# wo's last slice on 16 partitions by two loads, in a decode step of grouped-query attention with an MLP

## The chip, the cores and the metric

The kernel runs on one core of one Trainium2 chip. The metric is the device time of one execution in microseconds (us). Engines are named as the profile names them: PE (TensorE) with its weight loads PEld, DVE (VectorE), ACT (ScalarE), POOL (GpSimd) and SP, which here only issues transfers; 16 DMA engines move the data.

## The reference

One token x (512 values) goes through a layer norm, then through two branches whose results are added to x. All is float32.

```
xn = layernorm(x)
A:  q = xn @ wq                      # 32 heads of 128, wq 512 x 4096
    scores = q . k_cache * 128**-0.5  # 8 key heads, 65536 keys of 128 each; 4 query heads share one
    o = softmax(scores) @ v_cache
    a = concat(o) @ wo               # wo 4096 x 512
B:  b = relu(xn @ w1) @ w2           # w1 512 x 1792, w2 1792 x 512
out = x + a + b
```

k_cache and v_cache are 256 MiB each; wq and wo are 8 MiB each, w1 and w2 3.5 MiB each. All of it is read once.

## The kernel before

The arrays are laid out so that every transfer has long rows. SP issues all large loads, in this order: wq into the buffer `vs` in two loads, the first 8 MiB of k into the buffer `ks`; then in turn 8 MiB of v into `vs` and 8 MiB of k into `ks`, 32 of each (8 heads, four steps a head). A load waits until its buffer is free again: `k_free` is given by DVE when it has read the last score tile (L373), `v_free` by DVE when PE's sums of a step are complete (L396). While one buffer is computed on, the other is being filled.

When the last k buffer is free, w1 and w2 go into `ks`, still ahead of the last step's sums. When the last v buffer is free, wo goes into `vs`. wo is laid out with partition p = 16h + i (head group h, i from 0 to 15), and on each partition lie 32 slices of 512 values: slice j = 4r + g holds wo's row for head 4h + g and position 8i + r. `load_slices` cuts the 32 slices into loads of 16, 8, 4, 2, 1 and 1 (`WO`).

The end of the kernel is written out in order, with a semaphore for each engine (`Flow.op` waits for the marks that it is given, then issues). PE computes the MLP's hidden layer (L441), merges the heads (L451 to L464) and gathers w2 into acc_z (14 gathers). The attention output is spread by a matmul with `octet` (L483), masked and summed to `sw` (L485, L492): column j of `sw` holds, for each partition, the value that multiplies slice j. A *gather* (L503) is one matmul of a weight column with a row of 512; its result, one row, goes to one of four partitions of acc_z (0, 32, 64, 96, in turn), so that four gathers lie on four parts of the array.

acc_z's four rows must at the end become one, and the 512 results must go to four rows of 128 in acc_y, from which one transpose on DVE (L546) makes the layout of the output. Slices 0 to 27 (`DIRECT` is 28) are gathered in acc_z. Then DVE copies acc_z to `rows` (L534, called the fold's copy below). Slices 28 to 31 go straight into acc_y, four matmuls of 128 columns for each (L538). The fold's four matmuls with ones (L523) stand in PE's order behind slice 29, so that the copy runs beside the direct slices 28 and 29. After slice 31 the transpose and the output transfer follow.

On PE each of these matmuls shows as two instructions and two weight loads in the profile, so x8 in a row is four gathers, or one direct slice.

The functions that the change touches follow, with the line numbers of the profile.

Of the kernel before, what the change touches and what calls it, by code (L numbers as in the profile page):

```python
# [15 lines left out]
P = 128  # L16
D = 512
HQ, HKV, DH = 32, 8, 128
SK = 65536
DFF = 1792  # L20
G = HQ // HKV
CT = 4
# [12 lines left out]
R = HKV  # L35
SLICES = R * G
WQ = [4, 28]
WO = [16, 8, 4, 2, 1, 1]
DIRECT = 28
EPS = 1e-5  # L40

# [27 lines left out]
def attention_and_mlp_kernel(  # L69
# [30 lines left out]
    te, ve, se, ge, sy = nc.tensor, nc.vector, nc.scalar, nc.gpsimd, nc.sync  # L100

    def place(name, *shape, rows=P):
        return nc.alloc_sbuf_tensor(name, [rows, *shape], F32).ap()
# [9 lines left out]
    x4, yt = place("x4", P), place("yt", 32, 4)  # L113
    sw = place("sw", SLICES)
    mine = place("mine", HKV)
    octet = place("octet", P)
    eighth = place("eighth", R)

# [20 lines left out]
    rows = place("rows", 512)  # L139
# [10 lines left out]
    PE, DV, AC, GP = (Flow(nc, e, n) for e, n in ((te, "pe"), (ve, "dve"), (se, "act"), (ge, "pool")))  # L150

    def load(engine, name, dst, src, n=16):
        sem = nc.alloc_semaphore(name)
        engine.dma_start(dst, src).then_inc(sem, n)  # L154
        return sem, n


    def load_slices(name, src, counts):
        marks = []
        for n in counts:  # L160
            cut = slice(len(marks) * D, (len(marks) + n) * D)
            marks += [load(sy, f"{name}{len(marks)}", vs[:, cut], src[:, cut])] * n
        return marks
# [7 lines left out]
    tc.compile()  # L171


    make_identity_marks = []

    def memset(flow, ap, value):
        return flow.op(lambda e: e.memset(ap, value))

# [4 lines left out]
    for t in (acc_o, acc_z, pm):  # L183
# [9 lines left out]
        g0,  # L193
    )
    made = GP.mark
    x4_in = None
    se.wait_ge(*x4_free)
    x4_in = load(se, "x4_in", x4[0:P:32, :], x.rearrange("(c n) -> c n", c=CT))
# [43 lines left out]
            octet[:, : P // R].unsqueeze(1).to_broadcast([P, HKV - 1, P // R]),  # L242
        ),
        DV.mark,
    )
    DV.op(
        lambda e: e.tensor_mul(
# [4 lines left out]
    pz = pb[:, 1, :]  # L252
# [23 lines left out]
    for i in range(SLICES):  # L276
# [4 lines left out]
                start=(i < CT), stop=(i >= SLICES - CT),  # L281
# [34 lines left out]
    t1, t2 = ks[:, : A * DFF], ks[:, A * DFF : A * DFF + FB * D]  # L316
    w1_in = load(sy, "w1_in", t1, w1.rearrange("p a f -> p (a f)"))
    w2_in = load(sy, "w2_in", t2, w2.rearrange("p j n -> p (j n)"))
    sy.wait_ge(v_free, 1)
    wo_in = load_slices("wo", wo.rearrange("h (i r) g f -> (h i) (r g f)", r=R), WO)  # L320

# [14 lines left out]
    with nc.Fori(0, STEPS, engines=[ENG.PE]):  # L336
        te.wait_ge(k_in, 16).then_inc(k_in, -16)
        te.wait_ge(q_in, 1).then_inc(q_in, -1)  # L338
        for s in range(NT):
            tile_of = (pa, pb)[s // 2 % 2][:, s % 2, :]  # L340
            for c in range(CT):
                at = (s * CT + c) * TW
                i = te.matmul(tile_of[32 * c : 32 * c + 32, :], qcur, ks[:, at : at + TW], start=True, stop=True)  # L343
# [13 lines left out]
        for i in range(n):  # L357
# [5 lines left out]
                start=(i < CT), stop=(i >= n - CT),  # L363
# [4 lines left out]
    with nc.Fori(0, HKV, engines=[ENG.DVE], hint_back_edge=True, head_slot={ENG.DVE: 110}):  # L368
        for n in range(NP):
            for s in range(0, NT, 2):  # L370
                if s == NT - 2:

                    ve.wait_ge(s_tiles, NT // 2).then_inc(k_free, 1)  # L373
                i = ve.transpose(  # L374
                    tr[:, s * SUB : (s + 2) * SUB, :].rearrange("p b i -> p (b i)"),
                    (pa, pb)[s // 2 % 2].rearrange("p i k -> p (i k)"),
                )._wait_ge(s_tiles, s // 2 + 1)
# [5 lines left out]
            i = ve.reduce_max(top, tr[:, :, :G].rearrange("p b g -> p g b"), axis=AX.X)  # L383
            if n:
                ve.drain()
                i = ve.tensor_max(m, m, mc)  # L386
# [29 lines left out]
    with nc.Fori(0, HKV, engines=[ENG.Activation]):  # L416
        for n in range(NP):
            se.wait_ge(s_bias, 1).then_inc(s_bias, -1)  # L418
            for g in range(G):
                i = se.activation(  # L420
                    wt[:, :, g], tr[:, :, g], AF.Exp, bias=bias[:, n, g : g + 1],
                    scale=scale, accum_out=part[:, n, g : g + 1],
                )
# [13 lines left out]
    for a in range(A):  # L437
        for c in range(CT):
# [4 lines left out]
                    start=(a == 0), stop=(a == A - 1),  # L443
# [18 lines left out]
    for j in range(2):  # L462
# [28 lines left out]
    sw_in = DV.op(  # L491
        lambda e: e.reduce_sum(  # L492
            sw.rearrange("p (r g) -> p r g", r=R), spread.rearrange("p r h g -> p r g h"), axis=AX.X
        ),
        DV.mark,
    )

    begun = set()

    def gather(c, lhsT, row, marks, last=False):  # L500

        PE.op(
            lambda e: e.matmul(acc_z[32 * c : 32 * c + 1, :], lhsT, row, start=c not in begun, stop=last),  # L503
            *marks,
        )
        begun.add(c)
# [7 lines left out]
        )  # L514
    for j in range(FB):
        gather(j % CT, hT[:, j : j + 1], t2[:, j * D : (j + 1) * D], [hT_in, w2_in])

    for j in range(SLICES):
        if j == SLICES - 2:

            for c in range(CT):
                PE.op(
                    lambda e: e.matmul(  # L523
                        acc_y[32 * c : 32 * c + 1, :P], ones[:, 0:1], rows[:, c * P : (c + 1) * P],
                        start=False, stop=False,
                    ),
                    folded,
                )
        row = vs[:, j * D : (j + 1) * D]
        lhsT = sw[:, j : j + 1]  # L530
        if j < DIRECT:
            gather(j % CT, lhsT, row, [sw_in, wo_in[j]], last=(j >= DIRECT - CT))
            if j == DIRECT - 1:
                folded = DV.op(lambda e: e.tensor_copy(rows, acc_z), PE.mark)  # L534
        else:
            for c in range(CT):
                PE.op(
                    lambda e: e.matmul(  # L538
                        acc_y[32 * c : 32 * c + 1, :P], lhsT, row[:, c * P : (c + 1) * P],
                        start=False, stop=(j == SLICES - 1),  # L540
                    ),
                    sw_in, wo_in[j],
                )
# [40 lines left out]
```

## Time and profile before

| | us |
|---|---|
| median of 3 runs | 1303.35 (1303.03 to 1304.14) |
| the profiled execution | 1303.55 |
| its span, first to last instruction | 1302.2 |
| PE busy in it | 660.5 (51%) |
| DVE busy in it | 268.3 (21%) |
| ACT busy in it | 76.0 (6%) |
| bytes read from HBM in it | 560.99 MB, 431 GB/s over the span |

The mean granted clock of PE in this execution was 0.726 of full speed. In the rows below, times count from the first instruction of the span. A row of the timeline gives start, duration, engine, line, operation, output and inputs, shapes, the number of instructions merged in it, and in brackets the idle time of the engine before it with what ended it. A row of windows gives a stretch, its length, PE's busy time, PE's granted clock, the busy share of the 16 DMA engines and the GB/s that they moved. A row of a DMA queue gives its packets, its MB and the share of the 16 engines' time in that stretch.

### The profile page before, as it was taken

What the parts mean: (1) busy time and instruction counts of PE and PEld (TensorE: products, weight loads), DVE (VectorE), ACT (ScalarE), POOL (GpSimd) and SP (SyncE); (2) the same over time, 40 slices, a digit from 0 to 9 for tenths busy, and PEclk for the clock granted to TensorE, in tenths of its full rate; (3) what the DMA queues carried; (4) which work ended last, traced back from release to release, by engine and by line L of the source; (5) the groups of instructions that cost most, each with busy time, mean ns of one, the idle gap of its engine ahead of it and who ended that gap; (6) DMA issues with size and microseconds to landing.
All of it is one profiled execution on the core that took longest, in us unless ns stands there. A gap on an engine that the chain in (4) does not pass through costs nothing. (4 is left out here: it accounts for less than half of the span.)

```text
span 1302.2 us, 10668 instructions
## 1 busy us (share of the span) xinstructions
PE 660.5 (51%) x4512; PEld 184.9 (14%) x4512; DVE 268.3 (21%) x398; ACT 76.0 (6%) x292; POOL 4.1 (0%) x22
## 2 busy tenths in 40 slices
PE   3355455445445445546545535645544644544557
PEld 1111111111111111111111111111111111111111
DVE  2221122221122222012222112222112222201222
ACT  0000000000000000000000000000000000000000
POOL 0000000000000000000000000000000000000000
PEclk9677777687677677677667667677767767666768
DMA  9999999999999999999999999999999999999998
GB/s 417 421 443 425 445 425 439 431 425 445 423 447 421 449 419 445 425 445 425 433 437 425 445 421 449 421 447 421 445 425 439 431 431 439 423 447 421 449 416 360
DMA packets 10956, 561.06 MB, mean 431 GB/s; under 512 B 1476, under 2 KB 1480, under 8 KB 1864
## 3 DMA queue, kind: packets, MB, share of 16 engines
q1 hardware_dynamic: 10800, 561.00, 99.6%
q8 instruction: 3, 0.05, 0.0%
q10 hardware_dynamic: 152, 0.00, 0.0%
q14 instruction: 1, 0.01, 0.0%
HBM read 560.99 MB, written 0.00 MB: 431 GB/s over the span
## 5 line engine op out<-in xcount | busy, mean ns | idle before, releaser
L359 PE MATMUL acc_o<-vs,wt 128*16 128x512 f32 x2048 | 293.8, 738 | 178.9 <-PEq L355 178.9
L343 PE MATMUL pa<-ks,qcur 128*32 128x512 f32 x1024 | 175.7, 819 | 324.9 <-PEq L338 324.9
L374 DVE STREAM_TRANSPOSE tr<-pa 128x1024 f32<-128x1024 f32 x64 | 80.0, 1250 | 413.1 <-PE pa L343 413.1
L343 PE MATMUL pb<-ks,qcur 128*32 128x512 f32 x1024 | 139.6, 664 | 0.0
L420 ACT ACTIVATE wt<-tr,bias 128x128 f32<-128x128 f32 x128 | 64.3, 511 | 1083.7 <-ACTq L418 1083.7
L359 PEld LDWEIGHTS acc_o<-vs,wt 128*16 128x16 f32 x2048 | 69.0, 113 | 377.0 <-issue 377.0
L343 PEld LDWEIGHTS pa<-ks,qcur 128*32 128x32 f32 x1024 | 38.8, 134 | 432.7 <-issue 424.4
L400 DVE SCALAR_TENSOR_TENSOR acc<-acc,alpha,acc_o 128x512 f32<-128x512 f32 x24 | 17.9, 748 | 352.7 <-PE acc_o L359 352.7
L374 DVE STREAM_TRANSPOSE tr<-pb 128x1024 f32<-128x1024 f32 x64 | 80.0, 1250 | 49.6 <-PE pb L343 49.6
L343 PEld LDWEIGHTS pb<-ks,qcur 128*32 128x32 f32 x1024 | 41.6, 131 | 107.0 <-issue 87.9
L348 PE MATMUL pm<-ident,m 128*4 128x128 f32 x32 | 10.4, 324 | 87.7 <-DVE m L386 67.2
L398 DVE COPY acc<-acc_o 128x512 f32<-128x512 f32 x8 | 5.5, 691 | 119.3 <-PE acc_o L359 119.3
L349 PE MATMUL pm<-dg,ones 4*128 4x4 f32 x64 | 15.8, 316 | 21.3 <-DVE dg L390 21.3
L383 DVE TENSOR_REDUCE mc<-tr 128x4 f32<-128x512 f32 x24 | 24.1, 1006 | 1.8
L420 ACT ACTIVATION_READ_ACCUMULATOR wt<-tr,bias 128x1 f32 x128 | 23.9, 187 | 0.0
L348 PEld LDWEIGHTS pm<-ident,m 128*4 128x4 f32 x32 | 2.6, 81 | 116.7 <-DVE m L386 89.0
L349 PEld LDWEIGHTS pm<-dg,ones 4*128 4x128 f32 x64 | 13.0, 253 | 29.1 <-DVE dg L390 29.1
L350 PE MATMUL pm<-dg,rowg 4*128 4x1 f32 x64 | 15.1, 302 | 0.0
L279 PE MATMUL pa<-vs,tr 128*8 128x512 f32 x64 | 10.4, 809 | 8.6 <-DMA vs<-wq 7.3
L350 PEld LDWEIGHTS pm<-dg,rowg 4*128 4x128 f32 x64 | 13.9, 266 | 0.0
L388 DVE TENSOR_REDUCE mg<-pm 4x1 f32<-4x128 f32 x32 | 8.9, 279 | 13.3 <-PE pm L348 13.3
L391 DVE COPY bias<-pm 128x5 f32<-128x5 f32 x32 | 5.2, 163 | 29.5 <-PE pm L350 29.5
(98 smaller groups left out, 99.2 us busy)
## 6 DMA issues: line engine op xcount, KB each, us to landing
vs<-wq SPq DMA_DIRECT2D x1, 7168.0 KB, 21.2
ks<-w SPq DMA_DIRECT2D x2, 3584.0 KB, 21.8
vs<-wo SPq DMA_DIRECT2D x1, 4096.0 KB, 17.9
vs<-wo SPq DMA_DIRECT2D x1, 2048.0 KB, 22.4
vs<-wq SPq DMA_DIRECT2D x1, 1024.0 KB, 4.7
vs<-wo SPq DMA_DIRECT2D x1, 1024.0 KB, 24.4
ks<-k SPq DMA_DIRECT2D x32, 29.0
vs<-v SPq DMA_DIRECT2D x32, 28.9
```

Of the source, the lines that this page charges most:

```text
L279: lambda e: e.matmul(pr[32 * c : 32 * c + HKV, :], xs[:, i, :], vs[:, i * 512 : (i + 1) * 512], start=(i < CT), stop=(i >= SLICES - CT),),
L343: i = te.matmul(tile_of[32 * c : 32 * c + 32, :], qcur, ks[:, at : at + TW], start=True, stop=True)
L348: te.transpose(pm[:G, :P], m, ident)._wait_ge(s_dve, 3).then_inc(s_max, 1)
L349: te.matmul(pm[:, P : P + G], ones[:G, :], dg[:, :G], start=True, stop=True)._wait_ge(s_dve, 4)
L350: te.matmul(pm[:, P + G : P + G + 1], rowg, dg[:, G : G + 1], start=True, stop=True).then_inc(s_max, 1)
L359: mm = te.matmul(acc_o[32 * c : 32 * c + WIDE * G, :], wt[:, i * WIDE : (i + 1) * WIDE, :].rearrange("p b g -> p (b g)"), vs[:, i * 512 : ...
L374: i = ve.transpose(tr[:, s * SUB : (s + 2) * SUB, :].rearrange("p b i -> p (b i)"), (pa, pb)[s // 2 % 2].rearrange("p i k -> p (i k)"),)._ ...
L383: i = ve.reduce_max(top, tr[:, :, :G].rearrange("p b g -> p g b"), axis=AX.X)
L388: ve.reduce_max(mg, pm[:G, :P], axis=AX.X)._wait_ge(s_max, 1)
L398: ve.tensor_copy(flat, acc_o)
L400: ve.scalar_tensor_tensor(flat, flat, alpha[:, n : n + 1], acc_o, op0=ALU.mult, op1=ALU.add)
L420: i = se.activation(wt[:, :, g], tr[:, :, g], AF.Exp, bias=bias[:, n, g : g + 1], scale=scale, accum_out=part[:, n, g : g + 1],)
```

## The change

`WO` loses its last entry: 31 slices go into `vs`, in five loads. The 32nd slice (r = 7, g = 3) goes into a tensor of its own, `few`, of 64 partitions with eight rows of 512 on each. Two loads of eight partitions each fill it: load b takes, for head group h, the eight rows i = 8b to 8b + 7 of the slice and puts them on partition 32b + 4h. So partitions 0, 4, ... 28 and 32, 36, ... 60 hold 16 KB each; the others of the 64 stay zero from a memset on POOL. SP issues these two loads behind w2, ahead of the wait for `v_free`, after a wait for the memset.

The weights for `few` come from the last column of `sw`. POOL spreads it over eight columns (`swr`), PE moves it with a 64-column selection matrix `to_few` to the 16 partitions, and DVE copies the 64 x 8 result to `swf`. `to_few` is made at the start on POOL from `octet`. PE gathers `few` in eight gathers, one for each of the eight rows on a partition, behind slice 15 of wo and ahead of slice 16. Slices 28, 29 and 30 go straight into acc_y; the fold's matmuls stand between 28 and 29.

The diff, without the removal of an unused list and without the change of `stop=(j == SLICES - 1)` to `stop=(j == WHOLE - 1)`:

```diff
-WO = [16, 8, 4, 2, 1, 1]
+WO = [16, 8, 4, 2, 1]
+WHOLE = sum(WO)
+HALF = P // 2
...
     mine = place("mine", HKV)
+    to_few, swr, swf = place("to_few", HALF), place("swr", R), place("swf", R, rows=HALF)
+    few = place("few", R, D, rows=HALF)
...
     made = GP.mark
+    memset(GP, to_few, 0.0)
+    few_clear = memset(GP, few, 0.0)
...
+    GP.op(
+        lambda e: e.tensor_copy(
+            to_few.rearrange("p (b h f) -> p h b f", b=2, h=HKV)[:, :, :, 0],
+            octet[:, : P // R].rearrange("p (h b) -> p h b", b=2),
+        ),
+        DV.mark, GP.mark,
+    )
...
     w2_in = load(sy, "w2_in", t2, w2.rearrange("p j n -> p (j n)"))
+    sy.wait_ge(*few_clear)
+    last_rows = wo.rearrange("h (b i r) g f -> h b i r g f", b=2, r=R)
+    few_in = [
+        load(sy, f"few_in{b}", few[32 * b : 32 * (b + 1) : 4], last_rows[:, b, :, R - 1, G - 1, :]) for b in range(2)
+    ]
     sy.wait_ge(v_free, 1)
...
+    swr_in = GP.op(
+        lambda e: e.tensor_mul(swr, eighth, sw[:, SLICES - 1 :].to_broadcast([P, R])), sw_in
+    )
...
-    for j in range(SLICES):
-        if j == SLICES - 2:
+    at = 2 * P
+    PE.op(lambda e: e.matmul(pz[:HALF, at : at + R], to_few, swr, start=True, stop=True), swr_in)
+    swf_in = DV.op(lambda e: e.tensor_copy(swf, pz[:HALF, at : at + R]), PE.mark)
+
+    for j in range(WHOLE):
+        if j == 16:
+            for i in range(R):
+                gather(i % CT, swf[:, i : i + 1], few[:, i, :], [swf_in, *few_in])
+        if j == WHOLE - 2:
```

More of the change, by code (lines that the diff above doesn't have):

```diff
@@ L171, in attention_and_mlp_kernel @@
     tc.compile()
-    make_identity_marks = []
     def memset(flow, ap, value):
@@ L539, in attention_and_mlp_kernel @@
                         acc_y[32 * c : 32 * c + 1, :P], lhsT, row[:, c * P : (c + 1) * P],
-                        start=False, stop=(j == SLICES - 1),
+                        start=False, stop=(j == WHOLE - 1),
                     ),
```

## The prediction

> **What bounds the kernel now.** First the head of the page: span, the strip of the DMA engines, the HBM line.
>
> ```profile
> span 1302.2 us, 10668 instructions
> DMA  9999999999999999999999999999999999999998
> HBM read 560.99 MB, written 0.00 MB: 431 GB/s over the span
> ```
>
> The 16 DMA engines are nine tenths busy or more in every slice but the last, at 431 GB/s. The change moves the same bytes, so the stream's length stays; what can change is the order at the end of the stream and what follows the last landings. So the second view is the chain of waits that ended last (start, us, what), from the issue of wo's third load on.
>
> ```profile
> 1272.84 24.41 DMA vs<-wo
> 1297.25 0.04 issue
> 1297.30 1.16 PE acc_z L503 x8
> 1298.46 0.02 issue
> 1298.48 0.70 DVE rows L534
> 1299.18 0.04 issue
> 1299.23 0.40 PE acc_y L523 x8
> 1299.63 0.71 PE acc_y L538 x16
> 1300.34 0.02 issue
> 1300.36 0.41 DVE yt L546
> ```
>
> The end isn't set by the last load. It is set by the third (slices 24 to 27), which lands at 1297.25: four gathers (1.16), the fold's copy (0.70), its matmuls, the last two slices, the transpose. Each slice's matmul is two PE instructions, so x8 is four gathers. Third, the timeline of PE and its weight loads in that stretch, which tells how much PE has to spare.
>
> ```profile
> 1280.20 5.27 PE L503 MATMUL acc_z<-ks,hT 128*1 128x512 f32 x28 [1.16 <-DMA ks<-w]
> 1290.00 7.03 PE L503 MATMUL acc_z<-vs,sw 128*1 128x512 f32 x48 [4.53 <-DMA vs<-wo]
> ...
> 1294.80 0.10 PEld L503 LDWEIGHTS acc_z<-vs,sw 128*1 128x1 f32 x4 [0.42 <-DMA vs<-wo]
> 1295.13 0.10 PEld L503 LDWEIGHTS acc_z<-vs,sw 128*1 128x1 f32 x4 [0.23 <-issue]
> 1295.56 0.10 PEld L503 LDWEIGHTS acc_z<-vs,sw 128*1 128x1 f32 x4 [0.33 <-issue]
> 1295.99 0.10 PEld L503 LDWEIGHTS acc_z<-vs,sw 128*1 128x1 f32 x4 [0.33 <-issue]
> ...
> 1298.54 0.62 PE L538 MATMUL acc_y<-vs,sw 128*1 128x128 f32 x16 [0.20 <-DMA vs<-wo]
> ...
> 1299.34 0.21 PEld L538 LDWEIGHTS acc_y<-vs,sw 128*1 128x1 f32 x8
> 1299.81 0.10 PEld L538 LDWEIGHTS acc_y<-vs,sw 128*1 128x1 f32 x8 [0.27 <-DMA vs<-wo]
> ```
>
> Four weight loads (two gathers) come every 0.43 us: 0.215 us a slice. The first 24 slices run from 1290.00 in one piece. The weights of the second load's eight are the four rows from 1294.80 on (released by its landing); each stands one step ahead of its matmuls, which thus begin at 1295.13. Their last pair is issued at 1296.42, three steps of 0.43 on (with 0.6 us of matmul behind it the piece ends at 1297.03, as the row says), and PE is free for the next at 1296.85. The third load lets it go on at 1297.30: PE has 0.45 us to spare, no more. Fourth, the stretches that show the clock (PE busy, PEclk, DMA share, GB/s).
>
> ```profile
> 1285.00:1290.00 5.00, 0.47 (x4) 1.00 0.95 406
> 1290.90:1294.00 3.10, 3.10 (x20) 0.53 0.98 412
> 1294.00:1297.00 3.00, 3.00 (x32) 1.00 0.98 388
> 1298.00:1298.50 0.50, 0.34 (x4) 1.00 0.14 53
> 1298.65:1299.10 0.45, 0.45 (x16) 1.00 0.12 46
> ```
>
> After some 4.5 us of idleness PE's clock is granted at 0.53 for about 3.4 us, then at 1.00. And from 1298.0 on, the DMA share is 0.14 and 0.12, that is two engines of 16 (2/16 = 0.125): fourteen have finished, and every landing of wo waits for two late ones. Two views of the queues, the stretches 46 to 48 us and 1274.0 to 1276.5 us, each have one such row:
>
> ```profile
> q8 instruction: 1, 0.02, 3.0%
> ...
> q8 instruction: 1, 0.02, 2.7%
> ```
>
> 3.0% of 16 engines over 2 us is 0.96 us of one engine, 2.7% over 2.5 us is 1.08 us: a fetch of program code took an engine for about 1 us at each place. I estimate that these two engines are the late ones. No view names an engine by number.
>
> **The change part by part.** *Start.* POOL gets two memsets and one copy behind its own work.
>
> ```profile
> 0.25 0.10 POOL L574 MEMSET const-float32-0.0<- 128x1 f32 x1 [0.25 <-issue]
> ...
> 3.38 0.20 POOL L177 MEMSET ident<- 128x128 f32 x1 [2.93 <-POOLq L171]
> ...
> 11.11 0.27 DVE L240 COPY octet<-octet 128x112 f32<-128x112 f32 x1
> ...
> 22.69 8.56 PE L279 MATMUL pa<-vs,tr 128*8 128x512 f32 x56 [7.31 <-DMA vs<-wq]
> ...
> 33.28 0.19 POOL L327 COPY qcur<-qall 128x4 f32<-128x4 f32 x1 [29.17 <-DVE qall L288]
> ```
>
> One element costs 0.10, 128 cost 0.20; the 4096 of few cost between 3.3 us (0.10 + 4096 × 0.10/127) and 6.5 us (32 × 0.20). Even if every DVE instruction stood still for that time, PE's wait for wq (7.31 us) covers it; POOL then waits 29 us for qall, which hides the copy too. I take 0. Without that cover it would cost its 3.3 to 6.5 us. SP's wait for this memset comes 1250 us later and holds nothing.
>
> *SP's queue.* Two issues stand between w2's and the wait for v_free, and one fewer behind it.
>
> ```profile
> 1253.79 0.80 SPq L154 DMA_DIRECT2D ks<-w  x2
> 1271.99 2.70 SPq L154 DMA_DIRECT2D vs<-wo  x6
> ```
>
> Two issues take 0.80 us; from 1254.6 SP would then stay idle until 1271.99. Two more end at about 1255.4: nothing. The rest of wo is still issued at 1271.99.
>
> *The DMA order.* 256 KB now go before wo's first load, not behind its last. At 412 GB/s they take 262,144/412,000 = 0.64 us on all 16 engines, 1.27 us if only eight carry them. So wo's first five loads land later by between 0 (the late engines carry none of it) and 1.27 us (they are among eight that carry all of it); 0.64 if it is spread evenly. If none of it falls to the late ones they also lose their share of the old last load. The row nearest to a load onto few partitions is missing; I take 0, since only two engines of 16 set the landings, and the others have 1.1 us or more in hand (done by 1298.0, where the late ones still work at 1299.1), nearly the 1.27 that they could be given. Both ends stay in the range. A gain below zero on the first load is excluded, since nothing ahead of it is taken away.
>
> The Trainium skill, "DMA: Bandwidth & Descriptors", section "Why a DMA increments its semaphore by 16 and not by 1", says that a load uses at most as many engines as its outermost dimension has entries, the lowest-numbered first (eight here), and its section "The descriptor swizzle" gives engines 0 to 7 the partitions 0 to 63. By that the price is 1.27 us on those eight and 0 on the others; no run here shows the numbering.
>
> *The weights.* POOL's product (128x8), a 64x8 matmul and DVE's copy out of it come behind sw.
>
> ```profile
> 1278.01 0.70 PE L483 MATMUL pb<-tr,octet 128*128 128x256 f32 x2 [0.74 <-DVE tr L477]
> 1279.20 0.61 DVE L492 TENSOR_REDUCE sw<-tr 128x32 f32<-128x256 f32 x1
> ```
>
> sw ends at 1279.81, the product (0.2, as POOL's copy of 128x4 takes, to 0.6, as this reduction does) by 1280.4, while PE gathers w2 until 1285.47. The small matmul (at most 0.70) and the copy (at most 0.42, as a 128x256 one would take) end by 1286.6; the first wo matmul is at 1290.00. Nothing, with 3.4 us in hand. Were that gone, 1.1 us would be added.
>
> *Eight gathers from few, behind slice 15.* This is the step that costs. Slice 15's gathers end their issue at 1295.13. Eight more at 0.215 take 1.72, to 1296.85. The eight of the second load follow to 1298.57 (landed long before), and the four of the third, landed at 1297.25, are issued then: their end is 1298.57 + 1.16 = 1299.73, not 1298.46. The 0.45 us to spare is gone, and 1.72 - 0.45 = 1.27 us are on the path. If the clock were at half here, they would cost twice, 3.44; if PE had begun at full clock, its 3.4 us at 0.53 would give back about 1.6 us and the eight would be hidden. The phase of that dip isn't tied to the kernel by anything I see, so other executions may lie anywhere between; the profiled one already has a full dip, and I take it as it is.
>
> *The tail.* Fold 0.02 + 0.70 + 0.04, its matmuls, then two direct slices as before (29 and 30 for 30 and 31). The one direct slice less stands before the fold's matmuls, where PE has time anyway: 0. What goes is the wait for the last load: its weight loads stand at 1299.81, where 1299.34 + 0.21 + about 0.10 would be 1299.65. That saves 0.16.
>
> Sum: 1.27 + 0 - 0.16 = +1.1 us with the late engines spared. The profiled execution took 1303.55 us (span 1302.2 and 1.35 around it), so 1304.65; the median of the runs, 1303.35, lies 0.20 lower, so 1304.45, rounded to 1304.5. What is late next is PE itself, not a landing.
>
> **The rivals.**
> (a) *The late engines carry few.* Then the first load lands 1.27 later, PE starts 1.27 later, and both terms add: +2.4, 1305.7. For it: two of 16 engines, eight of which may carry the loads; nothing in the profile says on which side they are. Evenly spread, it is +1.75, 1305.1.
> The Trainium skill, "DMA: Bandwidth & Descriptors", section "Latency and other measured facts", says that engines 7 and 15 are usually the slow ones. That would put one late engine in each half and make (a) the case, 1305.7; in this trace the lag goes with two code fetches, and no row shows its engine.
> (b) *Hidden after all.* The dip of the clock ends before 1290.00, PE has 1.6 us more, the gathers fit, and the third load's landing rules as before: -0.16 to 0, 1303.3. For it: the dip's end at 1294 is an accident of one execution. Against it: PE was idle for 4.5 us just before, in each execution.
> (c) *Slower, beyond what can be told.* The change has no measurable effect within 0.2%, 2.6 us, about what a measurement of this kernel can tell; slower means above 1305.96. The place is the two loads: 128 rows of 2 KB, each eight to one partition, from places in HBM far apart. An engine at 412/16 GB/s takes 0.080 us for a row; sixteen rows on each of eight engines. With the late engines among them this case decides from 0.094 us a row (1.27 + 16 × 0.094 - 0.16 = 2.6); with the late ones spared, from 0.163 us (the others' 1.1 us in hand goes first). At twice the price, 0.16, and late engines in it: +3.7, 1307.0. For it: no row of this trace has such a shape. Against it: the old last load has rows of 2 KB as well, and at its place the stream still shows 388 GB/s.
> (d) *Faster by over 0.2%*: nothing found; the whole chain behind the third landing is 3.5 us.
>
> **How the numbers follow.** My forecast 0.50; (a) with the even spread 0.32, a fifth of which goes over 1305.96 by the spread of the runs; (b) 0.07; (c) 0.09; (d) 0.02. Faster 0.02; slower 0.09 + 0.06 = 0.15; same 0.83. The range reaches from a little below (b), 1303.0, to a little above (a), 1306.2, and leaves out (c), (d) and the edges. The likeliest one's own range is 1303.6 to 1305.2 (a dip half as deep; a landing of 0.6).
>
> **What the profile after would show.** Forecast: 72 PE instructions on acc_z from slice 0 to slice 27 without a DMA wait between them; a fold's copy that begins at about 1299.8 in the span; no DMA wait in the last direct slices; two issues of 128 KB. Rival (a): the first wo matmul at about 1291.3, not 1290.0. (b): a DMA wait before slice 24. (c): the same first matmul at 1292 or later. I am wrong if the fold's copy begins before 1298.6, or if SP, POOL or DVE at the start hold up the first scores at 42.9 us.

## The result, and the profile after

| | before | changed |
|---|---|---|
| median, us | 1303.38 (18 runs, 1302.88 to 1304.27) | 1305.45 (18 runs, 1304.57 to 1307.03) |
| profiled execution, us | 1303.55 (span 1302.2) | 1304.68 (span 1303.4) |

The ratio is 1.0016, with a 95% interval from 1.0009 to 1.0023: 2.07 us or 0.16% slower, clear of no change, but below the 0.2% that the prediction took as the bound of what can be told. The profiled execution of the changed kernel is one of its quicker ones, 0.77 under the median. So the trace explains the 1.13 us by which it differs from the one of before, and the rest had to be looked for in other runs.

The head of the page and the chain of waits that ended last, of the changed kernel:

```profile
span 1303.4 us, 10698 instructions
...
HBM read 560.99 MB, written 0.00 MB: 430 GB/s over the span
```
```profile
1271.34 18.62 DMA vs<-wo
1289.96 0.14 issue
1290.10 9.64 PE acc_z L523 x72
1299.73 0.02 issue
1299.76 0.70 DVE rows L560
1300.46 0.04 issue
1300.51 0.40 PE acc_y L549 x8
1300.90 0.56 PE acc_y L564 x16
1301.46 0.02 issue
1301.49 0.41 DVE yt L572
```

The stream moves the same bytes at the same rate. The chain has another form. Before, it hung on the landing of wo's third load (1297.25); now it hangs on the landing of the first (1289.96), and behind it 36 gathers run on PE without one wait for a transfer, to the fold's copy at 1299.76 (1298.48 before). The timeline of PE shows where the eight new ones (`few`) stand:

```profile
1290.10 5.00 PE L523 MATMUL acc_z<-vs,sw 128*1 128x512 f32 x32 [5.01 <-DMA vs<-wo]
...
1295.03 1.89 PE L523 MATMUL acc_z<-few,swf 64*1 64x512 f32 x16
...
1296.86 2.76 PE L523 MATMUL acc_z<-vs,sw 128*1 128x512 f32 x24
```

Before, PE was idle for 0.27 us between the row of 24 slices and the next, until the third load landed:

```profile
1297.30 1.04 PE L503 MATMUL acc_z<-vs,sw 128*1 128x512 f32 x8 [0.27 <-DMA vs<-wo]
```

Here the second and third load have landed before PE comes to them; no row shows a wait.

Stretches of the changed kernel (length, PE busy, PEclk, DMA share, GB/s):

```profile
1290.10:1292.90 2.80, 2.80 (x16) 0.50 0.94 401
1293.00:1296.00 3.00, 3.00 (x32) 1.00 0.96 397
1297.10:1297.80 0.70, 0.70 (x12) 1.00 0.64 252
1298.05:1298.30 0.25, 0.25 (x8) 1.00 0.13 49
```

PE's clock is at half for its first 2.8 us, at full after. The third row, read alone, misleads. A share of 0.64 would be ten engines of 16 at work, but the kernel before has nearly the same mean in the same stretch:

```profile
1297.10:1297.80 0.70, 0.50 (x8) 1.00 0.65 231
```

What differs is the course. Before, the share falls in steps of 0.2 us from 0.86 (1297.1 to 1297.3) to 0.32 (1297.7 to 1297.9). In the changed kernel it stays between 0.61 and 0.63 from 1296.9 to 1297.9 and then drops to 0.28: six engines have finished early, and some eight others finish together a microsecond later. From 1298.05 on it is two again, as before from 1298.0 on. That fits eight engines that carry the new loads, with the two late engines of before not among them; the reports of the engines, below, show it.

### The profile page after: what moved, and what is told of

Read it like the earlier page. It is cut to its first block, busy times and chain, and to the rows that moved or that the text cites. A ratio compares the mean times of both kernels' runs of the same rounds, so it can differ in the third digit from the quotient of the medians.

```text
span 1303.4 us, 10698 instructions
## 1 busy us (share of the span) xinstructions
PE 657.1 (50%) x4522; PEld 183.8 (14%) x4522; DVE 269.4 (21%) x399; ACT 75.9 (6%) x292; POOL 8.1 (1%) x26
```

## The experiments

Every kernel here was timed against the kernel before on the same chip; its median there was 1303.46 to 1303.54 us (27 to 33 runs). The others have 11 runs each. With 11 runs the 95% interval of a ratio reaches 0.0009, that is 1.2 us, to each side. A single difference below that is not clear of nothing by itself; several of the following lie there, and rest on more than one run or on the traces.

**The changed kernel once more.** No edit.

> The changed kernel as it is, a second time. The median of its 18 runs was 1305.45 us, 2.07 above before's 1303.38, but its profiled execution took only 1304.68, 1.13 above the one of before. Theory (PE bounds the end, and the length of the clock's dip behind its idle time varies from execution to execution): median about +2 us again, single times spread over 2 us or more, and in a profiled execution that took longer than 1304.68 the 36 gathers between the first wo load and the fold take longer than the 9.64 us seen there, by the same amount, with the first of them again at about 0.1 us behind the first load's landing. Rival (landings of wo vary, because the late DMA engines sometimes carry the new loads): the gathers start later, by up to 1.27 us, and take 9.6 us as before.

1305.45 us (1304.47 to 1306.10), ratio 1.0014 [1.0005, 1.0023]. Its profiled execution took 1305.45, the median itself. Its chain, and PE's clock in it:

```profile
1290.06 0.14 issue
1290.20 10.30 PE acc_z L523 x72
1300.50 0.02 issue
```
```profile
1290.20:1294.30 4.10, 4.10 (x20) 0.50 0.95 400
```

The gathers start 0.14 behind the landing, as in the first trace, but take 10.30 us and not 9.64, since the clock stays at half until 1294.3 and not until 1293. That is 0.66 of the 0.77 us between the two executions. The theory holds, with two executions as its evidence; the single times spread over 1.63 us, less than the 2 that it expected.

**The gathers of few first.**

```diff
-        if j == 16:
+        if j == 0:
             for i in range(R):
                 gather(i % CT, swf[:, i : i + 1], few[:, i, :], [swf_in, *few_in])
```

> The eight gathers of few stand ahead of slice 0, where PE idles from 1285 to 1290 us, not behind slice 15. The loads are the same. Theory (the eight gathers on PE's path are the loss): the fold's copy goes back to the third load's landing, 1298.5; 1303.2 us, 0.1 to 0.2 under before, about 2.2 under the changed kernel; PE waits for the third load again. Rival (the loads themselves delay wo): no more than 0.5 us under the changed kernel, 1304.9 or above.

1304.25 us (1303.39 to 1304.63), ratio 1.0004 [0.9995, 1.0013]. From PE's timeline:

```profile
1285.90 1.89 PE L523 MATMUL acc_z<-few,swf 64*1 64x512 f32 x16 [0.25 <-DVE swf L539]
1290.43 7.03 PE L523 MATMUL acc_z<-vs,sw 128*1 128x512 f32 x48 [2.64 <-DMA vs<-wo]
1297.83 1.04 PE L523 MATMUL acc_z<-vs,sw 128*1 128x512 f32 x8 [0.38 <-DMA vs<-wo]
```

The eight gathers now lie where PE idles, and PE waits 0.38 us for the third load again. That gives back 1.2 us, about the 1.27 of the prediction, where the theory expected 2.2. It does not go back to before: 0.8 us stay, and the rival that the loads delay wo has its share.

**Without the gathers of few.** In place of the eight gathers PE only waits for the two loads and for `swf`.

```diff
-            for i in range(R):
-                gather(i % CT, swf[:, i : i + 1], few[:, i, :], [swf_in, *few_in])
+            PE.need(swf_in, *few_in)
```

> The changed kernel without the eight gathers of few (the last slice's part of the output is left out); its loads, weights and waits stay. Theory (gathers on PE's path): 1303.2 us, as with the gathers first, since the landings did not move. Rival (loads delay wo): stays above 1304.5, since the loads are still there.

1304.11 us (1303.24 to 1304.81), ratio 1.0006 [0.9997, 1.0015]: the eight gathers behind slice 15 are worth 1.34 us, and 0.65 us stay without them. The time lies between what the two theories expected, so neither is enough alone. Its profiled execution was its quickest (1303.24) and is no picture of the 0.65.

**The slice ahead, but whole.** The kernel before, with the last slice taken in one load of 128 partitions at the same place and gathered once, behind slice 15.

```diff
+    few_in = load(sy, "few_in", few, wo.rearrange("h (i r) g f -> (h i) (r g f)", r=R)[:, (SLICES - 1) * D :])
     sy.wait_ge(v_free, 1)
...
+        if j == 16:
+            gather(0, sw[:, SLICES - 1 :], few, [sw_in, few_in])
```

> The kernel before with the last slice taken ahead of the wait for v_free in one load of 128 partitions, gathered in one gather behind slice 15: the order of the change without its eight rows on 16 partitions. All 16 DMA engines get 0.64 us of work ahead of wo, the late two as well. Theory (each landing of wo is set by the late engines, and the changed kernel spares them): the landings shift by 0.64, one gather costs 0.2 that PE has to spare, the wait for the last load (0.16) goes: +0.5 us, 1303.9. Rival (landings are not what sets the end): +0, 1303.3 or below.

1304.36 us (1303.70 to 1305.45), ratio 1.0007 [0.9998, 1.0016]: 0.9 above before, where 0.5 was expected. The sign is that of the theory, the size is not. Its profiled execution was its slowest (1305.45), and in it PE's clock was at half for long:

```profile
1291.05:1295.60 4.55, 4.55 (x24) 0.50 0.97 409
```

PE then ran without a wait from the first load's landing to the fold, so that the single added gather was on the path too. In how many of the executions that is so, one trace can't tell. The 0.64 us of the theory are in it: the two late engines finish the slice 0.61 and 0.63 us after their part of w2 (from the reports explained below). The rest of the 0.9 is thus argued from one trace.

**The loads away, and the loads doubled.** Both without the gathers. The first issues neither load; the second issues both again, into a tensor `more` that nothing reads.

```diff
-    few_in = [
-        load(sy, f"few_in{b}", few[32 * b : 32 * (b + 1) : 4], last_rows[:, b, :, R - 1, G - 1, :]) for b in range(2)
-    ]
+    few_in = []
```
```diff
+    few_in += [
+        load(sy, f"more_in{b}", more[32 * b : 32 * (b + 1) : 4], last_rows[:, b, :, R - 1, G - 1, :]) for b in range(2)
+    ]
```

> The changed kernel without the eight gathers of few and without its two loads (the last slice is left out of the output, and 256 KB are not read); memset, selection matrix, small matmul and copy stay. The kernel without the gathers alone took 1304.11 us, 0.65 above before. Theory (those 0.65 are the two loads, which make one more DMA engine late): 1303.3 us. Rival (they come from the new work on POOL, PE and DVE or from the order of the code): 1304.1.

> The changed kernel without the eight gathers (the last slice is left out of the output), with its two loads issued twice, the second pair into a tensor of its own that nothing reads: 512 KB ahead of wo. Theory (the loads put 1.27 us of work on eight DMA engines, and one of the eight has become the last to land): the first wo load lands 1.27 us later and the time is 1305.4 us. Rival (the eight are not the last; the late engines carry none of it): 1304.1 to 1304.5, as with one pair.

Without loads 1303.40 us (1302.62 to 1303.91), ratio 0.9999 [0.9990, 1.0009]: as before. So memset, selection matrix, product, small matmul and copy cost nothing that can be measured. With doubled loads 1305.82 us (1304.97 to 1306.71), ratio 1.0019 [1.0009, 1.0028]. In the order none, one pair, two pairs: 1303.40, 1304.11, 1305.82, or +0.71 and +1.71. The two ends are clear of each other; the middle step is smaller than its interval, but the traces show it too. PE's first wo matmul is at 1289.47 to 1290.00 in the four traces without a load ahead of wo (mean 1289.82), and at 1289.84 to 1290.58 in the six with one pair (mean 1290.22): 0.40 us later. The first wo matmul without loads and with two pairs:

```profile
1289.47 7.03 PE L521 MATMUL acc_z<-vs,sw 128*1 128x512 f32 x48 [4.32 <-DMA vs<-wo]
```
```profile
1291.48 8.41 PE L527 MATMUL acc_z<-vs,sw 128*1 128x512 f32 x56 [7.50 <-DMA vs<-wo]
```

2.0 us later with two pairs. In the second the gathers again run in one piece, so the later start also uses up what PE has to spare; that would be why the second pair costs more than its 1.27 us, which is argued and not tried. That the price is not even says that the eight engines first have something in hand. That was tried by itself:

**One load of the two.** Without the gathers; `for b in range(1)`.

> The changed kernel without the eight gathers and with only the first of its two loads (128 KB; the last slice is left out of the output). Without loads it took 1303.4 us, with both 1304.11, with both issued twice 1305.82: the second pair cost 1.7, the first 0.7. Theory (the eight engines that carry the loads first use up what they have in hand against the latest engines, some 0.6 us, before they set the landings): one load, 0.64 us on each of the eight, is nearly hidden, 1303.4 to 1303.6 us. Rival (the price goes by the bytes, or the latest engines are among the eight): 1303.8 us or more.

1303.48 us (1303.10 to 1304.27), ratio 1.0001 [0.9992, 1.0010]: no more than before, as the theory says. By the times, one load is hidden. The spans of the same runs are less clear (medians 1301.6 without loads, 1302.1 with one), so the runs alone don't settle it. The traces do.

**The reports of the engines.** Each DMA engine that carries part of a load adds to the load's semaphore when its part has landed, and the traces keep these times (the rows of the views print only the last). A load of 128 partitions has 16 such reports. Each load of `few` has one at its issue and then eight: it lies on eight engines. They fit together if each engine works off its part of the loads in order, so they can be followed from load to load.

Two engines trail from w2 on, in every trace. Without the gathers they report w2 at 1279.52 and 1279.53, while the first load of `few`, which comes behind w2, is complete at 1279.33: the two late engines carry none of it. But one of the eight trails as well. It reports the second load of `few` at 1279.99, the other seven by 1279.34. On each engine the first part of wo is reported about 9.7 us after the one ahead of it, so 1279.99 becomes 1289.70, and that is when wo's first load lands. Reports of wo's first load:

| run | loads of few | the later of the two late engines | the last of the eight |
|---|---|---|---|
| one load | 1 | 1289.89 | 1289.78 |
| without the gathers | 2 | 1289.24 | 1289.70 |
| changed kernel | 2 | 1289.57 | 1289.96 |
| changed kernel once more | 2 | 1289.56 | 1290.06 |
| loads doubled | 4 | 1289.70 | 1291.34 |

With one load the eighth engine lands 0.11 us ahead of the later late one, so the load is hidden. With two it is 0.39 to 0.50 us behind it (up to 0.58 in the other three traces with two loads), with four 1.64. So the price of the two loads is 0.4 to 0.6 us on wo's landings; the medians of the times gave 0.65 to 0.8.

The eighth engine trails since a code fetch of queue q14, about when w2 lands. In the changed kernel it is at 1277.7, ahead of both loads of `few`, and the eighth report of both is 0.67 to 0.69 late. With one load it is at 1280.1, when that load is complete (reports from 1279.06 to 1279.42, none late). With doubled loads it is at 1279.5: the eighth report is 0.06 and 0.11 late on the first pair, 0.39 and 0.50 on the second. The rows of the queue in 1277.6 to 1278.1, 1280.0 to 1280.5 and 1279.4 to 1279.9 of these three:

```profile
q14 instruction: 1, 0.01, 3.9%
q14 instruction: 1, 0.01, 3.9%
q14 instruction: 1, 0.01, 4.2%
```

3.9% of 16 engines over 0.5 us is 0.31 us of one engine. So the lag begins with this fetch in all three. No row names the engine, and why the lag is twice the fetch's own time is open.

**PE kept busy in its idle time.** 16 matmuls of hT and w2's rows (18 in the kernel before) into a bank that nothing reads any more, ahead of the wo loop.

```diff
+    for i in range(16):
+        c = i % CT
+        PE.op(
+            lambda e: e.matmul(
+                pm[32 * c : 32 * c + 1, :], hT[:, i % FB : i % FB + 1], t2[:, (i % FB) * D : (i % FB + 1) * D],
+                start=True, stop=True,
+            )
+        )
```

> The changed kernel with 16 more matmuls of hT and w2 rows into a PSUM bank that nothing reads any more, behind the small matmul with to_few: they fill PE's idle time from about 1285.4 to 1289 us. Theory (a part of the loss is the dip of PE's clock behind that idle time, which the 36 gathers now pay in full): the 36 gathers run at full clock, 36 x 0.215 = 7.7 us and not 9.6 to 10.3, PE waits again for the third load, and the time falls to that of the kernel without the gathers, 1304.1 us. Rival (the eight gathers cost what they cost at any clock): 1305.4, as before.

> The kernel before with 18 such matmuls at the same place. Theory (in it the gathers are hidden behind the landings even with the dip): 1303.4 us, no change. Rival (the dip costs the kernel before something as well, in the executions in which it is long): 1303.0 or less.

The kernel before: 1303.74 us (1303.16 to 1304.34), ratio 1.0002 [0.9992, 1.0011], no change, as expected. The changed kernel: 1304.80 us (1303.27 to 1305.91), ratio 1.0010 [1.0001, 1.0019], and this is inconclusive. The profiled execution took 1304.01 and does what the theory says:

```profile
1285.69 3.61 PE L544 MATMUL pm<-ks,hT 128*1 128x512 f32 x32
1290.58 3.61 PE L523 MATMUL acc_z<-vs,sw 128*1 128x512 f32 x32 [1.28 <-DMA vs<-wo]
1294.13 1.89 PE L523 MATMUL acc_z<-few,swf 64*1 64x512 f32 x16
```

16 slices take 3.61 us, not 5.00, and the fold waits for the third load. But only five of the 11 times lie at 1304.4 or below; the other six lie between 1304.80 and 1305.91, where the changed kernel lies without this edit. No trace of one of those was taken. One execution shows the gathers without the dip; how often these matmuls prevent it is open.

**The fold earlier.** `DIRECT = 24` in the kernel before and in the kernel with the gathers first: 24 slices in acc_z, the rest straight into acc_y.

> The kernel before with 24 slices in acc_z and eight straight into acc_y: the fold's copy no longer waits for the third load. Theory (before, the third load's landing sets the end, the last load's landing comes 0.15 us behind it): the last landing at 1299.8 sets the end, 0.1 to 0.15 us less, 1303.3 us. Rival (the eight direct slices, 32 small matmuls, hold PE up): 1303.8 or more.

> The changed kernel with the gathers of few ahead of slice 0 and 24 slices in acc_z, seven straight into acc_y. Theory (with the gathers off PE's path and the fold off the third landing, only the last landing is left, which no longer waits for the latest engines' share of the last slice): 0.5 to 0.8 us under the kernel with the gathers first (1304.25), 1303.4 to 1303.7 us, even with the kernel before. Rival (the fold was not on the path there): 1304.2.

The kernel before: 1303.46 us (1302.81 to 1304.12), ratio 0.9999 [0.9990, 1.0008]; the expected 0.1 can't be told from nothing at this spread. With the gathers first: 1303.59 us (1302.82 to 1304.35), ratio 1.0001 [0.9992, 1.0010], 0.66 under the same kernel with 28. Its chain:

```profile
1273.06 25.67 DMA vs<-wo
1298.73 0.04 issue
1298.77 0.40 PE acc_y L564 x8
1299.17 0.22 PE acc_y L549 x8
1299.39 0.56 PE acc_y L564 x16
1299.95 0.02 issue
1299.97 0.41 DVE yt L572
```

The fold's copy is no longer on it. With both edits no difference from the kernel before can be told, and no version was found that beats it.

## Why the prediction was right, and where it was off

The direction, the range (1303.0 to 1306.2) and the leaning to "same" held: 1305.45, ratio 1.0016. The single number, 1304.5, was 0.95 too low, and 1305.45 also lies outside the likeliest case's own range (1303.6 to 1305.2), between the two figures of rival (a), 1305.1 and 1305.7. The number alone would have spoken for (a); the traces don't. The main step was right, and two terms were too small.

*Eight gathers on PE's path, 1.27.* Right. The fold's copy begins at 1299.76 in the trace, where 1299.8 was forecast, PE has no wait for a transfer between slice 0 and slice 27, and the direct slices have none either. Taken away by itself the step is worth 1.34 us, moved into PE's idle time 1.2.

*"I take 0" for the order of the transfers.* This term failed. It is 0.4 to 0.6 us by the landings, 0.7 by the times (0.71 from the runs with none and with both). The premise that the late engines carry none of the loads was right, by the reports. The prediction had 1.1 us in hand against 1.27 us of new work, called that nearly the same, and took 0. The engine that counts had less: one of the eight was itself late by about 0.7 us, and had 0.7 to 0.9 in hand (1.27 less the 0.39 to 0.58 by which it overran). One load's 0.64 fits into that, two loads' 1.27 don't. The share of two engines at 1298.0 told how many were last; it did not tell how close the third was. The estimate that the fetches at 46 and 1274 us make the two late engines fits the reports: one engine trails on w1, which lands ahead of the second fetch, and two on w2, behind it.

*The profiled dip as it is.* The prediction took the dip of the trace for a full one and let other executions have less of it. The median has more: the changed kernel's first trace has 2.8 us at half clock behind the first landing, its second 4.1, and the second is the median. At half clock PE loses half of each such microsecond, so that is the 0.66 us between them.

*The sum.* The trace of the median execution and that of before are 1.90 us apart (1305.45 and 1303.55). PE starts on wo 0.20 later (1290.20 and 1290.00). From there to the fold's copy it takes 10.32 us and not 8.48, 1.84 more: 1.27 for the gathers, 0.35 for a dip that is 0.7 us longer than the 3.4 of before, and some 0.2 that no row separates. From the copy to the transpose it takes 1.73 us and not 1.88. That is 0.20 + 1.84 - 0.15 = 1.89. The first trace came out at +1.13, as forecast, by luck in part: its dip behind PE's start was 0.6 us shorter than before's, and its late engines were 0.3 us earlier (1289.57 and 1289.87), which hid most of the 0.39 us that the loads cost in it.

*The tail, -0.16.* Right: 1.73 us and not 1.88 from the copy to the transpose in both traces, and the direct slices have no wait in them.

*The start.* Right, and the cover was needed: POOL's memset of few took 3.50 us (forecast 3.3 to 6.5), and one DVE instruction beside it was held up.

```profile
4.16 3.50 POOL L179 MEMSET few<- 64x4096 f32 x1
...
22.77 8.07 PE L290 MATMUL pa<-vs,tr 128*8 128x512 f32 x56 [6.50 <-DMA vs<-wq]
```
```profile
6.59 1.10 DVE L208 TENSOR_SCALAR xc<-xT,st 128x4 f32<-128x4 f32 x1
```

PE still waits 6.50 us for wq, 0.81 less than before.

*The rivals.* (a) did not happen: the late engines do not carry few, though another engine of the eight became the last. The Trainium skill's remark in "DMA: Bandwidth & Descriptors", section "Latency and other measured facts", that engines 7 and 15 are usually slow finds no support here; no row names an engine, and the lags seen here start at code fetches. By the rule of the Trainium skill, same page, section "Why a DMA increments its semaphore by 16 and not by 1" a load of eight outer entries lies on eight engines, and with it the eight reports behind the issue agree. (b) is out: in both traces of the changed kernel itself the clock is at half when PE starts on wo. (c), dear rows, is out: on seven of the eight engines the second load of few is reported about 0.6 us after the first, in the changed kernel from 1278.78 to 1279.38, which is 0.075 us a row, where 0.080 was reckoned and 0.163 needed.

## What to carry to other kernels

Behind a stream that is bound by transfers, look at how much PE has to spare between the loads before putting work between them; here 0.45 us was all, and eight gathers that would have been free in an idle gap a few microseconds earlier cost 1.3. Loads onto a few partitions go to a few DMA engines, and each engine is a queue of its own: what counts is how late the latest of the engines that carry the load already is, and not how many are late. Where PE starts from idleness and bounds the end, take more than one trace of it, since the length of its clock's dip differs from execution to execution.

## What the runs showed of the hardware that was not expected

The two loads of eight rows on each of eight partitions take SP twice as long to issue as those of w1 and w2, 0.80 us each against 0.40, though they move 128 KB; nothing waited for it here.

```profile
1253.13 0.80 SPq L158 DMA_DIRECT2D ks<-w  x2
1253.98 1.61 SPq L158 DMA_DIRECT2D few<-wo  x2
```

A DVE instruction of four elements on each partition took 1.10 us beside POOL's memset, and 0.23 without it. It ended at 7.69, the memset at 7.66.

After a code fetch of 0.31 us one DMA engine was about 0.7 us late, and in the changed kernel it was as late in the last load of wo, 20 us later (1299.22, the other seven by 1298.55).

The time around the span is not constant: it is 1.35 us in the profiled execution of before, and between 1.3 and 2.0 in the others, 2.0 in that of the kernel before with PE kept busy (1304.34, span 1302.3). Whoever compares the spans of single executions alone does not see it.
